# 32-bit products of zeros in TensorE's idle time in the first part of an attention and feed-forward kernel

## The chip, the cores and the metric

The kernel runs on one core of one Trainium2 chip. The metric is the device time of one execution, in microseconds. A profiled execution gives the trace: what each engine did, and what ended each of its waits. The engines are TensorE (PE, with its weight loads as PEld), VectorE (DVE), ScalarE (ACT), GpSimd (POOL) and SyncE (SP). SP and POOL also issue the DMAs.

## What is computed

Eight batches of eight heads, each with 512 local tokens and 32 global ones, 64 wide. Global queries attend to all 544 keys, local ones to the 32 global keys and to local keys at a distance of at most 32. The result, as 4352 rows of 512, goes through a feed-forward layer with a gate.

```python
k_all = np.concatenate([k_g, k_l], axis=2)
v_all = np.concatenate([v_g, v_l], axis=2)
out_g = np.matmul(sm(scale * np.matmul(q_g, k_all.transpose(0, 1, 3, 2))), v_all)
s_ll = scale * np.matmul(q_l, k_l.transpose(0, 1, 3, 2))
mask = np.abs(pos[:, None] - pos[None, :]) <= window
s_ll = np.where(mask, s_ll, -1000000000.0)
s_lg = scale * np.matmul(q_l, k_g.transpose(0, 1, 3, 2))
out_l = np.matmul(sm(np.concatenate([s_lg, s_ll], axis=-1)), v_all)
...
h = x @ w_in
g = h * np.clip(h + 3.0, 0.0, 6.0) / 6.0
return (g @ w_out).astype(np.float32)
```

## The kernel before

The attention of a batch is cut into four local units (`local`, L594) and two global ones (`globe`, L703). A local unit goes through the engines in this order:

- TensorE computes scores in 32x32 tiles, 64 products in one operation of the plan (L628 for the first two batches, L615 for the others), into the PSUM tiles `s`, or `m` for every second unit of the first batch.
- VectorE adds the mask and takes the maximum, one 128x128 block at a time (L644), and ScalarE takes the exponential (L650).
- TensorE transposes the eight blocks (L659, into `t` or `m`), and ScalarE or VectorE copies them to `et` (L306, L308).
- TensorE multiplies by the values (L673) into the one PSUM tile `a` of two banks. The unit's two halves take the first 264 columns of one bank each.
- VectorE divides by the row sums (L681, L682), reading both banks of `a` and writing `x`. TensorE transposes `x` (L695), and a copy puts it into `xt`.

The global units do the same with other shapes (L723, L731, L737, L748, L757). The feed-forward part of a batch is `first` (L801, ScalarE's L813, VectorE's gate L808) and `second` (L830, copied out in L838 and stored by SP). For the first batch `first` works on halves of 256 columns.

The order of all this is not written out. `Plan` (L38) holds a stream of operations for each step, each operation with the engine, its cost in microseconds and what it depends on. `lay` (L118) picks the operation that can start first, breaks ties by rank, keeps a clock for each engine, and returns one list; the program is emitted in that order (L919), so it is the order of each engine's queue. The planner counts TensorE's instructions (`count`, from 60 on; `n` is what an operation adds, a weight load and a product being two), because the instructions come in blocks of 256 (`BLOCK`) and a block that has been asked for takes time to come (`FETCH`, `stalls`). `mode` tells full products from tiled ones; a switch between them is costed at 0.097.

`setup` (L343) is a row of memsets on VectorE, first the masks, then the edges of `kt`, the ones and zeros of `v`, `vg` and `vs`. POOL issues the loads and builds the masks, and some of its work waits for these memsets: the load of `vg` (L447, issued in L296) waits for the memset of L351.

The semaphores are placed by the framework, from what each instruction reads and writes in a tile.

Of the kernel before, what the change touches and what calls it, by code (L numbers as in the profile page):

```python
# [9 lines left out]
FP32 = mybir.dt.float32  # L10
# [3 lines left out]
class Buf:  # L14
# [4 lines left out]
    def __init__(self, pool, readers):  # L19
        self.pool, self.at, self.slot, self.left, self.free_at = pool, None, None, readers, 0.0  # L20
# [17 lines left out]
class Plan:  # L38
# [4 lines left out]
    BLOCK = 256  # L43
    FETCH = 2.5
    SWITCH, ALONE = 0.097, 1.0
    SPARE, PHASES = 0.3, 9

    def __init__(self, pools, claims):
        self.count, self.fetched, self.mode = 60, 0.0, "full"
        self.claims = claims  # L50
        self.tune = TUNE
        self.issued = {}
        self.free = {p: [0.0] * n for p, n in pools.items()}
        self.streams = {}
        self.rank = {}
# [62 lines left out]
    def lay(self):  # L118
        at = self.at = {n: 0 for n in self.streams}
        clock = {}  # L120
        order = []
        total = sum(len(s) for s in self.streams.values())
        while len(order) < total:
            found, lone = [], []
            for n, ops in self.streams.items():
                if at[n] == len(ops):
                    continue
                op = ops[at[n]]
                t = self.ready(op, n)
                if t is None:  # L130
                    continue
                for e, cost in op.on.items():
                    start = max(t, clock.get(e, 0.0))
                    rank = self.rank[n](at[n]) if callable(self.rank[n]) else self.rank[n]
                    rank += self.tune.get((n, at[n] * self.PHASES // len(ops)), 0.0)
                    if e == "PE":
                        cost += self.switch(op)
                        if self.stalls(op, start, op.on[e])[0] > 0.2:
                            rank += 20
                        if op.mode[0] != "full" and self.mode != "full":  # L140
                            rank -= 15
                        elif op.mode[0] != "full" and start - t < self.ALONE:
                            lone.append(len(found))
                    found.append((start, rank, start + cost, n, e))
            if not found:
                raise RuntimeError("no operation can be laid: " + ", ".join(f"{n} {at[n]}" for n in at if at[n] < len(self.streams[n])))
            if len(lone) == 1:
                start, rank, end, n, e = found[lone[0]]
                found[lone[0]] = (start, rank + 12, end, n, e)
            first = min(found)  # L150
            e = first[4]
            here = [f for f in found if f[4] == e and f[0] <= first[0] + 0.03]
            start, _, end, n, e = min(here, key=lambda f: (f[1], f[0]))
            op = self.streams[n][at[n]]
            if len(op.on) > 1:
                start, end, e = min(((f[0], f[2], f[4]) for f in found if f[3] == n), 
                                    key=lambda f: f[1] + (self.SPARE + self.tune.get(("spare " + n, at[n] * self.PHASES // len(self.streams[n])), 0.0)
                                                          if f[2] == "DVE" else 0.0))
            for b, p, i in self.choose(op, n)[1]:
                b.at, b.slot = p, i  # L160
                self.free[p][i] = None
            at[n] += 1
            if op.landing is not None:
                self.issued.setdefault(e, []).append(op.landing)
            if e == "PE":
                wait, when = self.stalls(op, start, op.on[e])
                end += wait
                self.mode = op.mode[1]
                if self.count % self.BLOCK + op.n >= self.BLOCK:
                    self.fetched = when + wait + self.FETCH + min(6.0, max(0.0, clock.get("DMA", 0.0) - when - 1.0))  # L170
                self.count += op.n
            clock[e] = end
            op.end, op.engine = end + op.lat, e
            for b in op.reads:
                b.left -= 1
                b.free_at = max(b.free_at, op.end)
                if b.left == 0:
                    self.free[b.at][b.slot] = b.free_at
            order.append((start, n, op))
        return order  # L180
# [3 lines left out]
def kernel(  # L184
# [12 lines left out]
    nc = tc.nc  # L197
    P = 128
# [37 lines left out]
    def tiles(name, n, shape, dtype, pool=None):  # L236
        return [(pool or sb).tile(shape, dtype, tag=f"{name}{i}", name=f"{name}{i}") for i in range(n)]
# [37 lines left out]
    qn, kn = w_out_t[2], w_out_t[3]  # L275
    gts = [tiles(f"gts{r}_", NDFF, [P, Sl], FP16) for r in range(2)]

    mps = tiles("m", 3, [P, 512], FP32, pp)
    sps = tiles("s", 2, [P, 512], FP32, pp)
    tps = tiles("t", 1, [P, 1024], FP16, pp)  # L280
    aps = tiles("a", 1, [P, 2, 512], FP32, pp)

    plan = Plan(sizes, {})
# [28 lines left out]
    def turned(t):  # L312

        return tps[t.slot] if t.at == "t" else mps[t.slot].bitcast(FP16)

    state = {b: {} for b in range(B)}
    units = []
    made = {}

    def quarter(e, f):  # L320
        return slice((2 * e + f) * W, (2 * e + f + 1) * W)

    def pairs(t):

        return t.rearrange("p (c s b) -> p c s b", c=NC, b=2)
# [15 lines left out]
            nc.gpsimd.memset(lines(kt[r])[:, :, at:at + W], 0.0)  # L341

    def setup():  # L343
        nc.vector.memset(masks, 0.0)
        for r in range(2):
            for e in range(2):
                nc.vector.memset(pairs(kt[r])[quarter(e, 0), :, 0:W, :], 0.0)
                nc.vector.memset(pairs(kt[r])[quarter(e, 1), :, LINE - W:, :], 0.0)
            nc.vector.memset(v0[r][:, :, :, D:D1], 1.0)
            nc.vector.memset(vg[r], 0.0)  # L350
            nc.vector.memset(vg[r][0:W, :, D:D1], 1.0)  # L351
            nc.vector.memset(vs[r][0:W, 0, 0, :, :], 0.0)
            nc.vector.memset(vs[r][P - W:P, NU - 1, NJ - 1, :, :], 0.0)
# [528 lines left out]

    with tc.manual_schedule():
        setup()
        g_first(0)
        loads(0, "l0")
# [64 lines left out]
```

## Time and profile before

| What | Value |
|---|---|
| Time, three runs | 341.26, 340.41, 340.36 us; median 340.41 |
| The profiled execution | 341.78 us, its span 340.0 us |
| Mean granted TensorE clock | 0.999 |
| Products, weight loads on TensorE | 4456, 4456 |
| DVE, ACT, POOL busy | 75%, 71%, 45% of the span |
| First score product, the 60 after it | at 9.45 us, from 12.60 us |
| First L801, first L830 | at 29.32 us, at 55.25 us |
| DMA in the 40 slices | nine tenths or more in 17 of the first 26 |

The page gives the busy time of each engine, then the span in 40 slices of 8.5 us. The view of waits names who waited for whom, with the total, the number of times and the longest. The timeline lists instructions in order of time: start, length, engine, line, operation, result and operands, how many, and in brackets the idle time before them with what ended it. "issue" there is time in which the engine waited for nothing that the profile shows. The view by windows gives, for each stretch, the busy time of PE, PEld, DVE, ACT and POOL with the number of instructions, then the granted clock, the DMA share and GB/s.

### The profile page before, as it was taken

How to read it: one execution, taken by the hardware profiler on the slowest of the kernel's cores; microseconds unless marked ns; L12 is line 12 of the kernel's file. 1: busy time of each engine (PE TensorE's matmuls, PEld its weight loads, DVE VectorE, ACT ScalarE, POOL GpSimd, SP SyncE). 2: the span in 40 equal slices, each digit the busy share in tenths (PEclk: the TensorE clock that was granted, in tenths of full speed). 3: DMA queues.
4: the chain of work that ended last, by engine and by line, in shares of the span. 5: the costliest groups of instructions: out<-in, count | busy, mean ns of one | idle time of the engine just before them, and what ended most of it. 6: DMA issues, size and time to landing. Idle time of an engine off the chain costs nothing.

```text
span 340.0 us, 11227 instructions
## 1 busy us (share of the span) xinstructions
PE 312.2 (92%) x4456; PEld 169.3 (50%) x4456; DVE 255.2 (75%) x955; ACT 241.0 (71%) x572; POOL 152.3 (45%) x184
## 2 busy tenths in 40 slices
PE   0458969899999999999999999999999999999995
PEld 0335756544455445545554555554545554445654
DVE  7777897759889699968997999799889864443310
ACT  5578969756897797769967996888779743443331
POOL 8488579407954974394529376715600000000000
PEclk9999999999999999999999999999999999999999
DMA  7989999999981996499729939993100000010112
GB/s 123 171 149 160 185 228 170 174 225 155 208 133 38 166 191 82 81 158 184 173 41 171 191 75 92 114 202 70 64 7 31 33 31 34 31 62 33 62 42 85
DMA packets 107077, 39.28 MB, mean 116 GB/s; under 512 B 92368, under 2 KB 100816, under 8 KB 107024
## 3 DMA queue, kind: packets, MB, share of 16 engines
q0 software_dynamic: 93536, 17.44, 64.6%
q1 hardware_dynamic: 13488, 21.12, 23.5%
q8 instruction: 35, 0.57, 0.7%
q14 instruction: 18, 0.15, 0.2%
HBM read 35.39 MB, written 8.91 MB: 130 GB/s over the span
## 4 chain that ended last, share of the span: by engine, by line
PE 87%; DVE 6%; issue 2%; DMA 2%; POOL 1%; ACT 1%; POOLq 0%; DVEq 0%
PE m L830 35%; PE m L801 33%; PE t L659 5%; PE a L673 3%; PE s L615 2%; PE t L695 2%; DMA wout<-in_k_l_dram 2%; DVE gts L808 2%; PE s L715 1%; PE t L748 1%; PE s L628 1%; PE a L757 1%; DVE sm L644 1%; DVE kt L525 1%; DVE x L682 1%
## 5 line engine op out<-in xcount | busy, mean ns | idle before, releaser
L830 PE MATMUL m<-wout,gts 128*128 128x512 f16 (+1 forms) x560 | 134.9, 373 | 0.6 <-issue 0.6
L801 PE MATMUL m<-xt,win 128*128 128x512 f16 (+1 forms) x576 | 126.3, 359 | 4.0 <-DVE gts L808 3.5
L808 DVE SCALAR_TENSOR_TENSOR gts<-t,m 128x512 f16<-128x512 f32 (+1 forms) x160 | 94.7, 603 | 41.0 <-ACT t L813 39.9
L813 ACT ACTIVATE t<-m 128x512 f32<-128x512 f32 (+1 forms) x160 | 84.2, 532 | 40.4 <-PE m L801 36.8
L477 POOL COPY vs<-v 32x1056 f32<-32x1056 f32 (+3 forms) x80 | 77.5, 968 | 42.9 <-DMA v<-in_v_l_dram 39.2
L650 ACT ACTIVATE ex<-sm,mx 128x128 f16<-128x128 f32 x256 | 86.2, 393 | 10.3 <-DVE mx L644 9.8
L801 PEld LDWEIGHTS <-win 128*128 128x128 f16 x640 | 60.0, 98 | 55.2 <-issue 5.1
L830 PEld LDWEIGHTS <-gts 128*128 128x128 f16 x560 | 51.2, 98 | 48.9 <-issue 2.3
L644 DVE CUSTOM_DVE_ANT_0 sm<-s,mask 128x128 f32<-128x128 f32 x240 | 56.6, 285 | 7.2 <-PE s L628 3.8
L838 ACT COPY ot<-m 128x512 f32<-128x512 f32 (+1 forms) x35 | 20.0, 571 | 16.6 <-PE m L830 16.4
L296 POOL DMA_DIRECT2D rawq<-in_q_l_dram x12 | 12.6, 1059 | 36.5 <-DVE qt L562 22.0
L296 POOL DMA_DIRECT2D v<-in_v_l_dram x32 | 28.2, 891 | 1.0 <-DMA win<-in_moe_w_in_dram 1.0
L306 ACT COPY et<-t 128x1024 f16<-128x1024 f16 x18 | 18.2, 1012 | 9.7 <-PE t L659 9.7
L682 DVE TENSOR_TENSOR x<-a,rec 128x512 f16<-128x512 f32 x32 | 22.1, 691 | 1.1
L644 DVE DVE_READ_ACCUMULATOR2_ANT mx<- 128x1 f32 x256 | 21.2, 83 | 0.0
L659 PE MATMUL t<-ident,ex 128*128 128x128 f16 x256 | 20.9, 228 | 0.0
L659 PEld LDWEIGHTS <-ex 128*128 128x128 f16 x256 | 17.5, 102 | 6.1 <-issue 0.5
L628 PE MATMUL s<-kt,qt 32*32 32x128 f16 x384 | 5.8, 246 | 13.0 <-DVE kt L533 9.4
L562 DVE STREAM_TRANSPOSE qt<-rawq 128x512 f16<-128x512 f16 x24 | 15.9, 691 | 0.0
L566 DVE STREAM_TRANSPOSE kt<-rawk 128x512 f16<-128x512 f16 x24 | 15.5, 682 | 0.0
L731 DVE TENSOR_REDUCE top<-s 128x1 f32<-128x288 f32 x32 | 13.0, 446 | 3.3 <-PE s L723 2.5
L673 PE MATMUL a<-vs,et 128*32 128x65 f16 x1024 | 14.3, 197 | 1.0 <-issue 0.9
(81 smaller groups left out, 250.4 us busy)
## 6 DMA issues: line engine op xcount, KB each, us to landing
out_dram<-ot SPq DMA_DIRECT2D x31, 256.0 KB, 2.1
vs<-vg SPq DMA_DIRECT2D x32, 132.0 KB, 6.2
v<-in_v_l_dram POOLq DMA_DIRECT2D x32, 128.0 KB, 6.9
rawq<-in_q_l_dram POOLq DMA_DIRECT2D x12, 256.0 KB, 5.9
rawk<-in_k_l_dram POOLq DMA_DIRECT2D x12, 256.0 KB, 8.0
rawq<-rawq SPq DMA_DIRECT2D x12, 254.0 KB, 6.8
rawk<-rawk SPq DMA_DIRECT2D x12, 254.0 KB, 6.1
win<-in_moe_w_in_dram POOLq DMA_DIRECT2D x8, 256.0 KB, 6.7
```

What stands on the lines that cost most here:

```text
L296: eng.dma_start(out=o() if callable(o) else o, in_=i() if callable(i) else i)
L477: (nc.gpsimd if op.engine == "POOL" else nc.vector).tensor_copy(out=o(), in_=i())
L644: nc.vector.tensor_tensor_reduce(out=sms[sm.slot], in0=scored(c // 2)[:, z:z + P], in1=masks[:, m, :], scale=-scale, scalar=3.0e38, op0=AL ...
L650: nc.scalar.activation(out=exs[ex.slot][:, un, c, :], in_=sms[sm.slot], func=EXP, scale=-1.0, bias=mxs[mx.slot])
L659: nc.tensor.matmul(out=turned(tp)[:, z:z + P], lhsT=exs[ex.slot][:, un, c, :], rhs=ident, is_transpose=True)
L673: nc.tensor.matmul(out=o[quarter(e, f), un, c, 0:D + 1], lhsT=ets[et.slot][:, un, c, quarter(e, f) if b >= WORDS else quarter(e ^ (c // 2) ...
L682: nc.vector.tensor_tensor(out=xs[x.slot], in0=o[:, :, :, 0:D], in1=recs[rec.slot].to_broadcast([P, 2, NC, D]), op=ALU.mult)
L801: nc.tensor.matmul(out=o if len(x.shape) == 2 else o.rearrange("p (a c) -> p a c", a=2), lhsT=w_in_t[c // 8][:, m, (c % 8) * P:(c % 8 + 1) ...
L808: nc.vector.scalar_tensor_tensor(out=g, in0=shape(t1s[t1.slot][:, 0:n]), scalar=1.0, in1=shape(mps[ps.slot][:, 0:n]), op0=ALU.min, op1=ALU ...
L813: r = plan.add("t1", Op(("ACT", 0.09 + n * 0.00083), lambda: nc.scalar.activation(out=t1s[t1.slot][:, 0:n], in_=mps[ps.slot][:, 0:n], func ...
L830: nc.tensor.matmul(out=mps[ps.slot][:, 0:n], lhsT=gfn(c), rhs=w_out_t[c // 4][:, c % 4, cols], start=(c == 0), stop=(c == NDFF - 1))
L838: nc.scalar.copy(out=o, in_=i)
```

## The change

A tile `busy` of 128x248 zeros in FP32 is added and set to zero by VectorE ahead of the other memsets. A product `filler` of 128x128 weights and 248 columns, both from `busy`, writes the last 248 columns of the second bank of `a`; nothing reads them. When the planner lays an operation on TensorE that starts before 36 us on its clock, it puts as many fillers ahead of it as fit into the idle time since the last one (from 2.5 us for the first), at 0.6 us each and by half of that less. They add two each to the count of instructions, and nothing to the clock.

```diff
+    FILL, FIRST, UNTIL = 0.6, 2.5, 36.0
...
+        self.filler = None
...
             if e == "PE":
+                idle = start - clock.get(e, self.FIRST)
+                for _ in range(int(max(0.0, idle - self.FILL / 2) / self.FILL) if self.filler and start < self.UNTIL else 0):
+                    order.append((start, "fill", Op((e, self.FILL), self.filler, n=2)))
+                    order[-1][2].engine = e
+                    order[-1][2].end = start
+                    self.count += 2
+                    total += 1
+                    self.mode = "full"
                 wait, when = self.stalls(op, start, op.on[e])
...
+    busy = tiles("busy", 1, [P, 248], FP32)[0]
...
+    def filler():
+
+        nc.tensor.matmul(out=aps[0][:, 1, 512 - 248:512], lhsT=busy[:, 0:P], rhs=busy, start=True, stop=True)
+    plan.filler = filler
...
     def setup():
+        nc.vector.memset(busy, 0.0)
         nc.vector.memset(masks, 0.0)
```

## The prediction

> **What bounds the kernel now.** First the page: busy time by engine and the row of the granted clock.
>
> ```profile
> PE 312.2 (92%) x4456; PEld 169.3 (50%) x4456; DVE 255.2 (75%) x955; ACT 241.0 (71%) x572; POOL 152.3 (45%) x184
> PEclk9999999999999999999999999999999999999999
> ```
>
> TensorE sets the end, and 28 of 340 us are left to win. The throttle's row never falls, so by it there is nothing to warm up. Next, TensorE's waits in the first 60 us; past them it loses only 1.8 us by name.
>
> ```profile
> PE s L628 <- DVE kt L533: 9.4, 1, 9.4
> PE m L801 <- DVE gts L808: 3.5, 4, 1.7
> PE m L628 <- issue: 2.9, 1, 2.9
> PE s L628 <- DVE kt L525: 2.9, 1, 2.9
> PE m L695 <- DVE x L682: 2.3, 2, 1.3
> ```
>
> Then TensorE's timeline to 48 us, where like is compared with like.
>
> ```profile
> 12.60 1.29 PE L628 MATMUL s<-kt,qt 32*32 32x128 f16 x60 [2.85 <-DVE kt L525]
> ...
> 21.14 0.79 PE L628 MATMUL m<-kt,qt 32*32 32x128 f16 x41 [2.87 <-issue]
> ...
> 23.53 0.61 PE L695 MATMUL m<-ident,x 128*128 128x128 f16 x4 [1.04 <-DVE x L682]
> ...
> 27.99 0.61 PE L695 MATMUL m<-ident,x 128*128 128x128 f16 x4 [1.27 <-DVE x L682]
> 28.40 1.06 PE L659 MATMUL t<-ident,ex 128*128 128x128 f16 x8
> 29.32 2.72 PE L801 MATMUL m<-xt,win 128*128 128x256 f16 x12
> 31.97 0.43 PE L673 MATMUL a<-vs,et 128*32 128x65 f16 x32
> ...
> 36.36 0.61 PE L659 MATMUL t<-ident,ex 128*128 128x128 f16 x8
> 47.27 1.47 PE L801 MATMUL m<-xt,win 128*128 128x256 f16 x12 [1.66 <-DVE gts L808]
> 48.67 0.74 PE L628 MATMUL s<-kt,qt 32*32 32x128 f16 x64
> ```
>
> Twelve products of 256 columns take 2.72 us at 29 us and 1.47 at 47; eight transposes 1.06, later 0.61; 64 score products 1.28, later 0.74. So the array runs at about half rate up to some 31.9 us, under a row that says 9. What ended that was 2.65 us of unbroken full-array products (29.32 to 31.97).
>
> Last, the same stretch in windows (TensorE busy first, the granted clock third from the end).
>
> ```profile
> 12.00:16.00 4.00, 2.69 (x145) 1.92 (x152) 3.02 (x21) 2.65 (x10) 0.48 (x1) 1.00 1.81 170
> 16.00:20.00 4.00, 2.27 (x91) 1.60 (x76) 3.88 (x25) 3.75 (x10) 2.20 (x4) 1.00 1.25 192
> 20.00:24.00 4.00, 1.82 (x78) 1.46 (x78) 2.17 (x8) 3.29 (x8) 3.74 (x7) 1.00 0.71 128
> 40.00:44.00 4.00, 2.45 (x59) 1.97 (x58) 3.93 (x10) 3.17 (x8) 3.83 (x5) 1.00 1.65 194
> 44.00:48.00 4.00, 2.26 (x20) 1.93 (x20) 3.96 (x13) 2.25 (x8) 2.21 (x4) 1.00 1.18 245
> ```
>
> Small score products and transposes at 57 to 67% busy left the rate low for 16 us; full-array products at about the same share (40 to 48 us) held it high. From 37 to 51 us VectorE is full, and from 51.4 on TensorE. The end therefore moves by as much as the VectorE and ScalarE work of 24 to 37 us moves.
>
> **The change, part by part.** Edits to the plan's count only move the order; its order may change after each 256-instruction boundary. The two later waits on "issue" (0.9 and 0.6 us) bound that: plus or minus 0.7, taken as 0.
>
> *How many.* The planner is part of the kernel. Laid for the kernel before, its own gaps ahead of TensorE operations up to 36 us are 9.64 (from 2.5), 1.15 ahead of the third scores, 1.31 ahead of the first L673, 1.56 and 1.42 ahead of the first two L695; by the diff's rule, (gap - 0.3)/0.6 cut to a whole number, that is 15 + 1 + 1 + 2 + 1 = 20 products, 40 instructions in its count.
>
> *One product's price.* No 32-bit product is in the trace. From below: an f16 product of 256 columns, 1.47/12 = 0.12 us high, 2.72/12 = 0.23 low. From above: the diff's own 0.6, and at half rate 0.6 x 2.72/1.47 = 1.1. I take 0.6, by which the gaps were counted; operands twice as wide on both sides would make 2 x 2 f16 passes, 0.49 high and 0.91 low, on either side of it.
>
> *The memset.* The 128x264-word memset takes 0.28 us, so `busy` (248 words) about 0.26, ahead of everything on VectorE. It is not covered: POOL waits for VectorE's last memset of `vg`, and its loads and masks lead to the second K load, on the chain.
>
> ```profile
> 3.23 0.60 POOL L296 DMA_DIRECT2D vg<-in_v_g_dram  x1 [0.44 <-DVE vg L351]
> 25.03 1.01 ACT L306 COPY et<-t 128x1024 f16<-128x1024 f16 x1 [1.67 <-PE t L659]
> ```
>
> It is +0.26 at the first scores (12.60 to 12.86).
>
> *The first 15* start when `busy` is zero, near 1.3 us, and need 15 x 0.6 = 9 us, ended by 10.3; if the first six go at 1.1, by 13.3. The cover is the 12.4 us of idle before 12.60. Without it, every product over costs its length. I take 0.
>
> *Scores 1 to 3, 12.9 to 16.9 us.* If the rate is high here, they end up to 0.5 us sooner each, but VectorE reads each 128x128 block at 0.21 us one behind the other from 13.98 to 18.0 without a gap, then TensorE runs into the stall. Worth 0.
>
> *The stall.* TensorE stops after 223 products, 446 instructions; with the 60 that the plan counts ahead of them, about two blocks of 256. Sixteen added products (32 instructions) put the stop 16 score products sooner. Its end is set by the arrival of the next block of instructions, asked for 256 instructions earlier: 15 score products earlier (0.3 us), less the 0.26. I take its end unmoved; bounds -0.3 and +0.3. The 16 products run after it: 16 x 1.28/64 = +0.3.
>
> *One product ahead of the first L673.* The plan knows of no stall; after it there is no gap: +0.6.
>
> *Two ahead of the first L695, one ahead of the second.* They write columns 264 to 511 of the bank of `a` whose first 264 columns VectorE reads in L681 and L682. If the dependency is kept by bank, they wait for L682's end, when L695 itself could start: nothing fills the 1.04 and 1.27 us, and each costs its whole length, +1.2 and +0.6. If by bytes, they are hidden and cost 0. The trace has no second user of a bank to tell; I take the wait, as the tile is one and its bank is one. Behind them queue L695, the next unit's transposes L659, scores and L673; VectorE's copy to `xt` and ScalarE's `et` wait for those. The Trainium skill, PSUM — Partial Sum Buffer, on bank collisions, says that TensorE and a reader must be kept apart by bank and quadrant, not by address; by it the wait is there, and no run shown so far can say.
>
> *The rate after the stall.* Fillers raise it, I take it, within their 9 us. But from 13 to 28 us the array does what left it low before, with a few fillers in it and a stall of 2.87. I take it lost by 21 us. Nothing then gets shorter.
>
> *Sum.* To the second L695: 0.3 + 0.6 + 1.2 + 0.6 = +2.7. ScalarE is full from 25.03 to 38.6 but for idle of 0.27, 0.38 and 0.18; these 0.83 take up the delay. +2.7 - 0.83 = **+1.9 us** at 37 us, carried through VectorE's full stretch to the end. The profiled run took 341.78 us (span 340.0), 1.37 over the median of three; on that scale 343.7, on the median's 340.41 + 1.9 = **342.3**.
>
> **The rivals.**
>
> *The rate holds to 32 us, the fillers wait.* For: 40 to 48 us held it at 57 to 61% busy, and the stall is short. Against: that was full-array work. With the 0.49 of the high rate a product, after the stall: first L673 0.2 less, L695 0.2 less, L659 0.4 less, remaining scores 0.2 less, three fillers 1.47 more: +0.5 at ScalarE's 25.03; the second L695, L659 and the 12 products of L801 give 0.2 + 0.4 + 1.2 less and a filler 0.49 more, 1.3 less in all, but ScalarE's 0.83 of idle is all that can shrink: 0.5 - 0.83 = -0.3. About 340.1, no change. The Trainium skill, TensorE: Matmul & The Clock Gate, Part 1, gives this rule: full rate after about 3.4 us of activity, lost only after an idle window of that length. The 2.65 us at 29.32 agree with its rise; for its hold, the 2.87 us stall is too short.
>
> *The same, and the fillers are free* (hidden behind L682, or a fraction of 0.6). At 25.03 then -0.2 - 0.2 - 0.4 - 0.2 + 0.2 = -0.8, and -0.83 after it: -1.6, 338.8. For: the gaps are there. Against: the shared bank.
>
> *More than two instructions each.* With four, the stop comes 32 products sooner, after 191, so L659's eight transposes (ScalarE's `et` at 17.86) fall behind it. Then ScalarE starts `et` near 22.0 and has 1.01 + 0.40 + 1.92 + 1.57 + 0.63 to do before 25.03: 27.5, +2.5; with a filler wait on top and 0.83 off, some +2.9: 343.3. It decides from about 24 instructions more than planned (192 + 8 products done).
>
> *Zeros raise nothing.* Fifteen at 1.1 end at 17.8 in place of 12.86; the block is asked for later, too: +4, 344.5.
>
> **Chances.** Forecast 0.42; more instructions 0.13; zeros 0.05; rate held, waiting 0.20; rate held, free 0.20. About 0.3% (1.0 us) is what can be told from no change. Slower: 0.36 of the forecast, 0.13, 0.05 and 0.02 of the held rate: 0.56. Faster: 0.18 of the free case, 0.05 of the waiting one, 0.02 of order luck: 0.25. Same: 0.19. The forecast's own range is 340.8 (fillers at 0.23) to 344.2 (at 1.1). The range of 8 in 10 takes in most of the free case and the instruction case: 338.8 to 344.3.
>
> **What would show it.** Right: L659 at 1.06 and L801 x12 at 2.7 after 21 us as before; a filler starting at the end of L682 and L695 behind it; "issue" ending near 21.1. Wrong: L801 x12 at 1.4 from its first; fillers inside the gaps; a stall that ends elsewhere or a second one; a faster run with ScalarE's `et` before 25.0.

## The result

The changed kernel takes 1.0083 times the time of the kernel before, 95% interval 1.0056 to 1.0109: on the 340.41 us of the runs shown before, about +2.8 us. In eleven runs of each on one chip the medians are 344.14 and 341.09 us. It is slower, as forecast; the forecast was +1.9 us, 342.3, with a range of 338.8 to 344.3. The profiled execution took 345.36 us, its span 343.6.

In the changed kernel the lines are 17 further down: L645 is the scores (L628 before), L676 the transposes (L659), L690 the products with the values (L673), L699 the division (L682), L712 the transposes of `x` (L695), L818 and L847 the feed-forward products (L801, L830). L329 is the added product. The order of the other TensorE instructions is, product for product, that of the kernel before, in this kernel and in all the experiments.

First two rows of the page of the changed kernel, TensorE's busy time and the granted clock:

```profile
PE 324.0 (94%) x4496; PEld 178.8 (52%) x4496; DVE 255.4 (74%) x956; ACT 240.7 (70%) x572; POOL 152.3 (44%) x184
PEclk9756899999999999999999999999999999999999
```

TensorE is busy for 12 us more. It has 40 more products and 40 more weight loads, not 20: each 32-bit product is two of each, four instructions. And the clock row now shows a dip in its second to fifth slices.

TensorE's timeline of the changed kernel, to the first L847 (start, length, instructions, and the idle time before them with its cause):

```profile
1.18 8.69 PE L329 MATMUL a<-busy 128*128 128x248 f32 x30 [1.18 <-DVE busy L360]
...
14.98 1.19 PE L329 MATMUL a<-busy 128*128 128x248 f32 x2
16.11 1.05 PE L645 MATMUL s<-kt,qt 32*32 32x128 f16 x63
21.14 0.26 PE L645 MATMUL s<-kt,qt 32*32 32x128 f16 x1 [3.98 <-issue]
21.33 1.03 PE L676 MATMUL t<-ident,ex 128*128 128x128 f16 x8
...
23.28 1.20 PE L329 MATMUL a<-busy 128*128 128x248 f32 x2
24.41 0.63 PE L690 MATMUL a<-vs,et 128*32 128x65 f16 x32
26.08 2.02 PE L329 MATMUL a<-busy 128*128 128x248 f32 x4 [1.04 <-DVE x L699]
27.90 0.63 PE L712 MATMUL m<-ident,x 128*128 128x128 f16 x4
...
32.38 0.74 PE L329 MATMUL a<-busy 128*128 128x248 f32 x2 [1.47 <-DVE x L699]
32.92 0.63 PE L712 MATMUL m<-ident,x 128*128 128x128 f16 x4
...
34.23 2.47 PE L818 MATMUL m<-xt,win 128*128 128x256 f16 x12
...
59.92 2.75 PE L847 MATMUL m<-wout,gts 128*128 128x512 f16 x12
```

In the kernel before, the transposes and 23 more score products come ahead of the stall:

```profile
16.79 1.03 PE L659 MATMUL t<-ident,ex 128*128 128x128 f16 x8
17.75 0.52 PE L628 MATMUL m<-kt,qt 32*32 32x128 f16 x23
```

Three things stand here. The stall ends at 21.14, as before, but starts after 191 products of the kernel's own, all of them scores, and not after 223 (215 of scores and the eight transposes), so the eight transposes L676 lie behind it. The 32 products that are missing are the 30 and the 2 of the added ones ahead of the stall. The idle time of 1.04 us ahead of L712 is where it was, and the added products follow it. And L690, L712 and L676 take the long times of the kernel before (0.63, 0.63, 1.03). The second L712 starts at 32.92 (27.99 before), the first L818 at 34.23 (29.32 before), the first L847 at 59.92 (55.25 before): 4.7 us late at the start of the stretch that TensorE fills.

The windows of the changed kernel (TensorE's busy time first, the granted clock third from the end):

```profile
2.17:5.58 3.41, 3.41 (x10) 2.80 (x9) 2.70 (x16) 1.45 (x3) 2.58 (x11) 1.00 0.82 134
8.99:12.40 3.41, 1.05 (x9) 0.64 (x8) 2.35 (x7) 1.02 (x5) 3.41 (x6) 1.00 1.77 193
12.40:15.81 3.41, 2.97 (x126) 2.10 (x125) 2.44 (x17) 2.27 (x9) 0.34 (x1) 0.50 1.80 172
26.06:29.47 3.41, 3.39 (x24) 2.69 (x32) 2.18 (x13) 1.88 (x7) 3.41 (x6) 0.50 1.04 158
29.47:32.88 3.41, 1.25 (x50) 0.70 (x35) 2.73 (x14) 3.38 (x10) 2.27 (x3) 1.00 1.05 159
32.88:36.30 3.42, 3.42 (x23) 2.80 (x22) 1.87 (x10) 2.35 (x6) 1.63 (x2) 0.50 1.23 205
```

The trace's records of the clock change at 5.58 (up), 12.40 (down), 29.47 (up), 32.88 (down) and 36.30 (up for good); the windows are cut at these points. The products ahead of the scores raise the clock, and it falls 0.4 us before the first block of scores begins in earnest (12.78).

The longest waits of TensorE in the first 60 us of the changed kernel:

```profile
PE s L645 <- issue: 4.0, 1, 4.0
PE m L818 <- DVE gts L825: 3.6, 4, 1.7
PE s L645 <- DVE kt L542: 2.7, 1, 2.7
PE a L329 <- DVE x L699: 2.5, 2, 1.5
```

The waits for L699 are now those of the added products, not of L712: they wait for the same thing as the instruction behind them.

### The profile page after: what moved, and what is told of

Its sections match the earlier page's. It is cut to its first block, busy times and chain, and to the rows that moved or that the text cites. A ratio compares the mean times of both kernels' runs of the same rounds, so it can differ in the third digit from the quotient of the medians.

```text
span 343.6 us, 11308 instructions
## 1 busy us (share of the span) xinstructions
PE 324.0 (94%) x4496; PEld 178.8 (52%) x4496; DVE 255.4 (74%) x956; ACT 240.7 (70%) x572; POOL 152.3 (44%) x184
## 4 chain that ended last, share of the span: by engine, by line
PE 87%; DVE 6%; issue 2%; DMA 2%; POOL 1%; ACT 1%; POOLq 0%; DVEq 0%
PE m L847 35%; PE m L818 33%; PE t L676 5%; PE a L690 3%; PE s L632 2%; PE t L712 2%; DMA wout<-in_k_l_dram 2%; DVE gts L825 2%; PE a L329 1%; PE s L732 1%; PE s L645 1%; PE t L765 1%; PE a L774 1%; DVE kt L542 1%; DVE x L699 1%
## 5 line engine op out<-in xcount | busy, mean ns | idle before, releaser
L847 PE MATMUL m<-wout,gts 128*128 128x512 f16 (+1 forms) x560 | 134.9, 373 | 0.0
L818 PE MATMUL m<-xt,win 128*128 128x512 f16 (+1 forms) x576 | 126.0, 358 | 4.0 <-DVE gts L825 3.6
L830 ACT ACTIVATE t<-m 128x512 f32<-128x512 f32 (+1 forms) x160 | 84.2, 532 | 40.2 <-PE m L818 36.6
L818 PEld LDWEIGHTS <-win 128*128 128x128 f16 x640 | 60.0, 99 | 55.1 <-issue 5.1
L847 PEld LDWEIGHTS <-gts 128*128 128x128 f16 x560 | 51.2, 98 | 48.4 <-issue 1.8
L699 DVE TENSOR_TENSOR x<-a,rec 128x512 f16<-128x512 f32 x32 | 22.1, 691 | 1.1
L676 PEld LDWEIGHTS <-ex 128*128 128x128 f16 x256 | 17.5, 102 | 10.3 <-issue 4.9
L676 PE MATMUL t<-ident,ex 128*128 128x128 f16 x256 | 20.9, 228 | 0.0
L329 PE MATMUL a<-busy 128*128 128x248 f32 x40 | 13.9, 506 | 3.7 <-DVE x L699 2.5
L317 ACT COPY xt<-t 128x512 f16<-128x512 f16 x23 | 13.4, 584 | 2.2 <-PE t L712 2.1
```

The costliest lines, as they stand in the source:

```text
L317: nc.scalar.copy(out=o(), in_=i())
L676: nc.tensor.matmul(out=turned(tp)[:, z:z + P], lhsT=exs[ex.slot][:, un, c, :], rhs=ident, is_transpose=True)
L699: nc.vector.tensor_tensor(out=xs[x.slot], in0=o[:, :, :, 0:D], in1=recs[rec.slot].to_broadcast([P, 2, NC, D]), op=ALU.mult)
L818: nc.tensor.matmul(out=o if len(x.shape) == 2 else o.rearrange("p (a c) -> p a c", a=2), lhsT=w_in_t[c // 8][:, m, (c % 8) * P:(c % 8 + 1) ...
L830: r = plan.add("t1", Op(("ACT", 0.09 + n * 0.00083), lambda: nc.scalar.activation(out=t1s[t1.slot][:, 0:n], in_=mps[ps.slot][:, 0:n], func ...
L847: nc.tensor.matmul(out=mps[ps.slot][:, 0:n], lhsT=gfn(c), rhs=w_out_t[c // 4][:, c % 4, cols], start=(c == 0), stop=(c == NDFF - 1))
```

## The experiments

Each kernel is timed against the kernel before on the same chip; ratios are with 95% intervals. Single profiles differ by about a microsecond ahead of 20 us, with the landing of the second K load: the 60 scores started between 11.58 and 12.82 us in kernels where only that load held them. Three kernels have the same TensorE instructions up to 44 us: the kernel before, the one with the memset alone and the one with 40 small products near 45 us. In their profiles the stall ends at 21.14, 20.91 and 20.38, and the first product of the second feed-forward layer starts at 55.25, 55.70 and 53.97. So a difference of a microsecond or two between two profiles shows nothing by itself; the ratios do.

### The 15 products ahead alone

```diff
-    FILL, FIRST, UNTIL = 0.6, 2.5, 36.0
+    FILL, FIRST, UNTIL = 0.6, 2.5, 13.0
```

> Only the 15 products ahead of the first scores (60 instructions), none in the later gaps. Theory (each product is four instructions, so the stop for the next block comes 30 score products sooner, ahead of the eight transposes L659): 'issue' from about 16.9 to 21.1 us, the first copy to et at 22.2 to 22.5 instead of 17.9, the second L695 some 2 us later than in the kernel before (28.0), the end +1 to +2.5 us over before. Rival (only the products in the gaps cost, since the 15 end at 9.9 us, ahead of the scores): within 0.5 us of before.

Ratio 1.0036 (1.0010 to 1.0063), some +1.2 us, against the rival. In TensorE's timeline of this kernel the stop comes after one of the eight transposes:

```profile
16.09 0.29 PE L676 MATMUL t<-ident,ex 128*128 128x128 f16 x1
20.94 0.90 PE L676 MATMUL t<-ident,ex 128*128 128x128 f16 x7 [4.56 <-issue]
```

The first copy to `et` starts at 21.88, the second L712 at 30.24. Products that end at 10.5 us, ahead of all but the first four scores, cost 2 us of delay at 30 us.

### The same instructions without the array's work

```diff
-        nc.tensor.matmul(out=aps[0][:, 1, 512 - 248:512], lhsT=busy[:, 0:P], rhs=busy, start=True, stop=True)
+        half = busy.bitcast(FP16)
+        for _ in range(2):
+            nc.tensor.matmul(out=aps[0][0:W, 1, 512 - P:512], lhsT=half[0:W, 0:W], rhs=half[0:W, 0:P], start=True, stop=True)
```

(with `UNTIL` at 13.0, as above)

> In place of each of the 15 first products two f16 products of 32x32 by 128 columns, so 30 products and the same 60 instructions, with little array time and, I take it, no rise of the granted clock. Theory (instructions count, not the array's time): stall, et and end as in the run with only the first 15, within 0.7 us. Rival (the array's work or the clock's rise and fall costs): as the kernel before, within 0.5 us.

Ratio 1.0054 (1.0029 to 1.0078), as with the 15. The small products leave the clock down until 32.4 us, and the stop again falls after one transposition. Neither the array's time nor the clock's rise and fall is what the 15 cost, but their 60 places in the instruction stream.

### A whole block of instructions ahead

```diff
-    FILL, FIRST, UNTIL = 0.6, 2.5, 36.0
+    FILL, FIRST, UNTIL = 0.85, 2.5, 13.0
...
+    ahead = []
...
+        half = busy.bitcast(FP16)
+        for _ in range(0 if ahead else 108):
+            nc.tensor.matmul(out=aps[0][0:W, 1, 512 - 16:512], lhsT=half[0:W, 0:W], rhs=half[0:W, 0:16], start=True, stop=True)
+        ahead.append(1)
         nc.tensor.matmul(out=aps[0][:, 1, 512 - 248:512], lhsT=busy[:, 0:P], rhs=busy, start=True, stop=True)
```

(at 0.85 us each, ten 32-bit products fit in place of 15)

> Ahead of the first scores 108 small f16 products and then ten of the 32-bit ones, 216 + 40 = 256 instructions, none in the gaps. Theory (the place of the stop counts, not the products): a whole block is added, so TensorE stops after 223 products of the kernel again, L659 is done before, the first et at about 18, the second L695 at 28 to 28.5, the end within 0.6 us of before, though the clock is raised ahead of the scores and falls as with the 15. Rival (the rise and fall, or the array's work, costs): +1 us or more, as with the 15 alone.

Ratio 0.9994 (0.9960 to 1.0028): the cost is gone. The timeline of this kernel:

```profile
15.90 0.62 PE L681 MATMUL t<-ident,ex 128*128 128x128 f16 x8
16.45 0.44 PE L650 MATMUL m<-kt,qt 32*32 32x128 f16 x23
20.93 0.79 PE L650 MATMUL m<-kt,qt 32*32 32x128 f16 x41 [4.04 <-issue]
```

The stop is after 223 products again. Here the clock was up from 9.4 to 19.7 us, by its records, and scores and transposes took little more than half their time (0.62 for eight transposes against 1.03). What they saved went into the stall: 4.04 us for 2.87, ending within 0.2 us of where it did. The raised clock was worth nothing in this stretch.

### The five products in the gaps alone

```diff
-    FILL, FIRST, UNTIL = 0.6, 2.5, 36.0
+    FILL, FIRST, UNTIL = 0.6, 12.0, 36.0
```

> Only the five products in the later gaps (20 instructions). Theory (the product ahead of the first L673 and the three ahead of L695 run in front of what they precede, 0.83 us each at the low rate; the stop comes only two products sooner, so L659 is in time): the second L695 at 28.0 + 3.3 = 31.3 us, the end +1.5 to +2.5 us. Rival (the loss of the change is the block of instructions alone): +0.5 us or less.

Ratio 1.0070 (1.0041 to 1.0099), some +2.4 us: the larger part of the loss. The timeline of this kernel:

```profile
25.00 2.02 PE L329 MATMUL a<-busy 128*128 128x248 f32 x4 [1.04 <-DVE x L699]
26.82 0.63 PE L712 MATMUL m<-ident,x 128*128 128x128 f16 x4
```

VectorE's L699 starts at 24.26 and takes 0.69. The second L712 starts at 31.83, 3.8 us after that of the kernel before.

### The five products into a free PSUM tile

```diff
+                    spot = next((p, i) for p in ("t", "s", "m") for i, x in enumerate(self.free[p]) if x is not None and x <= start)
...
-    def filler():
+    def filler(spot):
...
+        to = {"t": tps[0].bitcast(FP32), "s": sps[0], "m": mps[spot[1]]}[spot[0]]
+        nc.tensor.matmul(out=to[:, 0:248], lhsT=busy[:, 0:P], rhs=busy, start=True, stop=True)
```

(on top of the edit above; the plan finds `t` free all five times)

> The five later products alone again, but into a PSUM tile that the plan has free, not into the bank of a that VectorE reads. Theory (they wait for L682 because of the bank): they start at the end of TensorE's work before, and the three ahead of L695 are hidden but for 1.66 - 1.04 = 0.6 us; second L695 at about 28.0 + 0.83 + 0.6 = 29.4, the end +0.3 to +1 us, at least 1 us below the run with the same five in the bank of a. Rival (the bank isn't what holds them, the queue is): the same as that run.

Ratio 0.9986 (0.9966 to 1.0007). In its timeline the four passes follow L692, the products with the values, at once:

```profile
22.69 0.63 PE L692 MATMUL a<-vs,et 128*32 128x65 f16 x32
23.25 2.02 PE L331 MATMUL t<-busy 128*128 128x248 f32 x4
25.07 0.63 PE L714 MATMUL m<-ident,x 128*128 128x128 f16 x4
```

The second L714 starts at 29.19, 2.6 us sooner than with the same products in `a`. Part of that is the clock, by its records up from 18.82 to 22.24 and from 25.65 us on here, and from 28.92 there. From the start of the products with the values to the first L714, at the low rate in both, it is 2.38 us here and 3.49 there (23.33 to 26.82): the 1.1 us are the wait. Writing into `a` is what held the products; the run changes the tile and the bank at once, so it does not tell which of the two the dependency is kept by. By the ratios, the two runs with these five products differ by more than the whole loss of the gaps. The end is a little better than forecast, since the raised clock stayed: L820 took 1.47 us for its first 12 products.

### The memset alone

```diff
-        nc.tensor.matmul(out=aps[0][:, 1, 512 - 248:512], lhsT=busy[:, 0:P], rhs=busy, start=True, stop=True)
+        pass
```

> The memset of busy stays and the plan counts its 20 products, but none is issued. Theory: the order of TensorE's instructions is that of before; the memset moves the first scores by at most 0.3 us and the end of the stall, the arrival of a block, by less; the end within 0.4 us of before. Rival (the memset's 0.26 us on the chain is carried through): +0.26 us, which this many runs can hardly tell from nothing.

Ratio 0.9993 (0.9956 to 1.0030): nothing that can be seen. As its TensorE instructions are those of the kernel before, its profile also shows what changes by itself. Its later waits on "issue" are this one alone, 0.61 us, where the kernel before has 0.85 + 0.57:

```profile
64.34 0.30 PE L690 MATMUL a<-vs,et 128*32 128x65 f16 x15 [0.61 <-issue]
```

### Moving the later stops

The changed kernel is 4.67 us late at the first L847 and only 3.6 at the end of the span, and its waits on "issue" after that point are 0.36 us, not 0.85 + 0.57. That looked like the merit of its 80 added instructions.

```diff
-        for _, _, op in plan.lay():
+        more = 40
+        for start, _, op in plan.lay():
+            if op.engine == "PE" and start > 43.0:
+                for _ in range(more):
+                    nc.tensor.matmul(out=aps[0][0:W, 1, 512 - 16:512], lhsT=busy, rhs=busy[:, 0:16], start=True, stop=True)
+                more = 0
             op.emit()
```

(on the kernel before, with a `busy` of 32x32 zeros in f16)

> The kernel before, with 40 small f16 products (80 instructions) put into TensorE's idle time near 45 us and no 32-bit ones. Theory (the change gets part of its loss back since its 80 instructions move the later stops for a block, 1.4 us in the kernel before and 0.4 in the changed one): the first 45 us as before, the later waits on issue 0.5 us or less in all, the end -0.7 to -1.2 us. Rival (the later waits have another cause, or the products take their place): within 0.4 us of before, or slower.

Ratio 1.0032 (0.9995 to 1.0070): the theory fell. The products filled the idle time near 45 us as meant, but of the later waits on "issue" in its timeline one grew:

```profile
61.84 0.36 PE L630 MATMUL s<-kt,qt 32*32 32x128 f16 x23 [0.37 <-issue]
69.14 0.81 PE L832 MATMUL m<-wout,gts 128*128 128x512 f16 x3 [2.79 <-issue]
```

The same number of added instructions gives 0.36 us of later stalls in a kernel that is 4.7 us late and 3.16 in one that is on time. So the place of a stop alone does not set its length. What ends it can be read from the packets of the instruction queue (q8, 16 KB each): in the kernel before and the changed one such a packet ends at 19.64 and 19.71 us, and in all 13 profiles each of the 33 waits on "issue" of TensorE's products ends 1.1 to 1.7 us after one. What sets when a packet moves was not tried by itself; the DMA traffic of the moment is a guess.

### Three products in a free tile, and the later stops

```diff
-                for _ in range(int(max(0.0, idle - self.FILL / 2) / self.FILL) if self.filler and start < self.UNTIL else 0):
+                for _ in range(int(max(0.0, idle - self.FILL / 2) / self.FILL) if self.filler and n == "xp" and start < self.UNTIL else 0):
...
+        more = 34
```

(on top of the free tile, which leaves two fillers ahead of the first L695 and one ahead of the second, and with the loop of the last experiment)

> Three 32-bit products alone, two ahead of the first L695 and one ahead of the second, into a free PSUM tile, and 34 small ones near 45 us (12 + 68 = 80 instructions). Theory: without the ones ahead of the scores and of L673 nothing is late ahead of 24 us; the products ahead of L695 fill idle time, but for some 0.6 us of the first two, and may raise the clock by 29 us; the later stops are moved as in the run with 40 small products: the end -1 to -2 us. Rival (the clock stays low, and the 0.6 us goes through): -0.5 us or less.

Ratio 1.0097 (1.0060 to 1.0135), the slowest of all, and against the theory. Up to 54 us it is as forecast: second L714 at 27.95, first L849 at 53.95. But the kernel with the 40 small products, which has none in the gaps and whose stall ends at the same time (20.38, here 20.36), is there at 53.97. Its lines, and then those of this kernel:

```profile
28.57 2.18 PE L803 MATMUL m<-xt,win 128*128 128x256 f16 x12
30.68 0.43 PE L675 MATMUL a<-vs,et 128*32 128x65 f16 x32
...
29.28 1.47 PE L820 MATMUL m<-xt,win 128*128 128x256 f16 x12 [0.49 <-ACT xt L318]
30.68 0.43 PE L692 MATMUL a<-vs,et 128*32 128x65 f16 x32
```

In these two profiles the raised clock wins back what the three products cost, and no more. Then come waits on "issue" of 1.21 and 2.52 us, and the second one does more than delay. The windows of this kernel around it:

```profile
66.90:70.31 3.41, 0.89 (x5) 0.29 (x3) 1.31 (x4) 0.98 (x3) 0.00 (x0) 1.00 0.96 245
70.31:73.72 3.41, 3.41 (x18) 2.02 (x17) 0.00 (x0) 1.49 (x4) 0.00 (x0) 0.50 0.76 182
```

With TensorE idle for 2.5 of 3.4 us the clock fell, and the next window ran at half.

### Versions from these parts

The three products ahead of L695 in the free tile, without the small ones at 43 us:

> Only the three products ahead of the first two L695, into a free PSUM tile (12 instructions); nothing ahead of the scores and nothing near 45 us. Theory: second L695 no later than before but for 0.6 us, the clock raised by about 26 to 29 us, L801 x12 at 1.5 us; the end 0 to -1.5 us. What differs from the run with 34 small products near 45 us, +1.0% there, is then the later waits on issue (3.7 us there). Rival (the three products themselves cost): slower than before by 1 us or more.

Ratio 0.9970 (0.9941 to 0.9999). The same with 108 small and ten 32-bit products, one block, ahead of the scores:

```diff
-        for _, _, op in plan.lay():
+        order = plan.lay()
+        zero = busy.bitcast(FP16)
+        for _ in range(108):
+            nc.tensor.matmul(out=aps[0][0:W, 1, 512 - 16:512], lhsT=zero[0:W, 0:W], rhs=zero[0:W, 0:16], start=True, stop=True)
+        for _ in range(10):
+            nc.tensor.matmul(out=aps[0][:, 1, 512 - 248:512], lhsT=busy[:, 0:P], rhs=busy, start=True, stop=True)
+        for _, _, op in order:
             op.emit()
```

> The change with both of its costs taken out: a whole block of 256 instructions ahead of the scores (108 small products and ten 32-bit ones), and in the gaps only the three ahead of the first two L695, into a free PSUM tile. Theory (a raised clock has little to win here, since ahead of 21 us VectorE and the stall set the pace and behind it ScalarE): no stall or wait worse than in the kernel before up to 50 us, the twelve products of L801 near 29 us at 1.5 instead of 2.7 us, the end 0 to -1.5 us. Rival (the raised clock is worth what TensorE's busy time loses, some 5 us): -3 us or more.

Ratio 0.9961 (0.9936 to 0.9987): the change with both its costs taken out, and with them two of its five products in the gaps, is a little faster than the kernel before. In its timeline the second L714 and the first L820 show the raised clock:

```profile
28.25 0.40 PE L714 MATMUL m<-ident,x 128*128 128x128 f16 x4 [0.74 <-DVE x L701]
29.58 1.47 PE L820 MATMUL m<-xt,win 128*128 128x256 f16 x12 [0.49 <-ACT xt L318]
```

L820 now waits for ScalarE, and starts no sooner than before (29.32): its 12 products are 1.2 us shorter than in the profile of the kernel before, and 0.7 shorter than in that of the kernel with 40 small ones. The two versions can't be told apart, so the part ahead of the scores is not shown to be worth anything; where their 0.3 to 0.4% comes from is open. With 101 small products ahead in place of the block (`range(101)`, and no 32-bit ones there):

> The three products ahead of L695 in a free tile and 101 small ones (202 instructions) ahead of the scores, so that the stop moves from 223 to about 250 products, 27 score products later, and is asked for as much later. Theory (end of the stall set by when the block is asked for, 27 score products at 20 ns): stall begins 0.5 us later and ends 0 to 0.5 us later; up to 50 us -0.5 to 0 against the run without them; what the later waits on issue do can't be told ahead, so the end within 2 us of it either way.

Ratio 1.0006 (0.9978 to 1.0034). The stop did move to 250 products, and the stall shrank to 2.02 us. But it ended at 20.36, 1.3 us sooner than without the small products (21.67), where the theory had the same time or later. With profiles that differ by about as much, this does not bear the theory out, and does not refute it. Later waits of 0.92 and 1.41 us took back what was won.

### What the profiles add up to

The first feed-forward product of the second layer (L830 before), the span from it to the end, and the waits on "issue" in that span, from the profiles:

| Kernel | First L830 | From it to the end | Later waits on issue | Difference |
|---|---|---|---|---|
| before | 55.25 | 284.8 | 1.42 | 283.3 |
| changed | 59.92 | 283.7 | 0.36 | 283.3 |
| 15 ahead | 57.46 | 283.4 | 0.28 | 283.1 |
| five in gaps | 58.89 | 284.0 | 0.60 | 283.4 |
| five in gaps, free tile | 55.20 | 284.4 | 1.10 | 283.3 |
| whole block | 55.71 | 285.2 | 1.98 | 283.2 |
| memset alone | 55.70 | 283.9 | 0.61 | 283.3 |
| 40 small at 43 us | 53.97 | 286.4 | 3.16 | 283.3 |
| three, free tile, 34 small | 53.95 | 288.7 | 3.73 | 284.9 |
| block and three, free tile | 54.25 | 285.3 | 1.97 | 283.3 |
| three, free tile | 54.69 | 284.7 | 1.37 | 283.4 |

From the first L830 on, every kernel takes 283.1 to 283.4 us and its later stalls (the two not shown 283.2 and 283.0); the one exception is the kernel whose clock fell at 70 us, by 1.6. So the time is set by two things: when the second layer starts, and how long TensorE waits for instructions after it. The changed kernel is 4.67 us worse in the first and 1.06 better in the second, 3.6 in its span. The second is not shown to be the change's doing: the kernel with the memset alone is 0.81 better there, too, with the TensorE instructions of the kernel before.

## Why the prediction was right, and where its terms were off

- *Half rate under a row that says 9.* Right, and now seen in the records: the first one of the kernel before is the rise at 32.03 us, and the row counts the time ahead of the first record as full. In the changed kernel, too, it is 1.00 in the window 2.17 to 5.58, where a pass of the 32-bit product takes 0.41 us.
- *The first 15 end in time.* Right: at 9.87, before the scores.
- *The rate is lost by 21 us.* Right, and sooner than thought: at 12.40, ahead of the 60 scores. So what lost it was not the small scores and the stall, as the prediction had it, but the idle time behind the added products (1.05 us busy from 8.99 to 12.40); scores and stall come later.
- *Fillers wait for L682 and run in front of L695.* Right; the run in the free tile shows that writing into `a` is the cause, though not whether tile or bank counts. The Trainium skill, PSUM — Partial Sum Buffer, on bank collisions, asks for a separation by bank, and the trace fits it: 1.04 us of idle with the product in the bank of `a`, none in another.
- *One product's price, 0.6.* Mis-sized. Four passes take 2.02 us and two 1.20 at the low rate, so a pass is 0.41 and a product 0.82; at the high rate 19 passes took 4.1 us, 0.43 a product. The terms of the four products between the stall and the second L695 were 0.6 + 1.2 + 0.6 = 2.4 us; at these prices they are 0.82 + 1.65 + 0.43 = 2.9. In the timeline what stands behind them starts 1.13, 1.82 and 0.54 us after they do, 3.5 in all.
- *Two instructions each.* This is the step that failed. "Sixteen added products (32 instructions) put the stop 16 score products sooner" was 64 instructions and 32 products, as the rival with 0.13 had it: a stop after 191. So L659 fell behind the stall. That rival's mechanism is the one that ran, and its 343.3 is the figure nearest to the result (340.41 x 1.0083 = 343.2), although ScalarE's second `et` came at 29.42 and not at its 27.5. In the forecast the term was +0.3; the 15 alone, with no filler behind them, put the second L695 2.2 us late, and with a whole block ahead, L659 in front of the stall again, that delay was gone. The delay there was +2.7 in the sum and 4.9 in the trace.
- *ScalarE's idle 0.83 takes up delay.* Wrong: 4.93 us late at the second L695, 4.67 at the first L830; 2.25 and 2.21 for the 15 alone. Those gaps end with transposes and products that are just as late: in the changed kernel ScalarE still waits 0.32 and 0.35 us there, and 0.40 more for L712.
- *Carried to the end.* In the two profiles 1.1 us of the delay came back, as the later stalls fell from 1.42 to 0.36; the forecast allowed 0.7 either way. Most of that can be chance, as the memset alone shows (0.61).
- So that +1.9 came near +2.8 is in part luck. The delay at 37 us was over twice the forecast, 4.9 us in the profile; at the end the profiles differ by 3.6 and the runs by 2.8, and nothing in the sum stands for what was lost on the way.
- *The memset and the stall's end.* Right within what can be seen: 21.14 in both profiles, where equal instructions gave 20.38 to 21.14, and the memset alone gives no difference.

## What to carry to other kernels

Count a filler in instructions before you count it in time: ahead of a stop for instructions, each one moves useful work behind it, even in time that is idle. A filler must not write into a PSUM tile that another engine is still reading, or it waits for the very thing that made the gap and then stands in front of the work. Compare a profile with a second one of the same instructions before reading a microsecond in it. And ask what the faster engine waits for next: where another engine or the stream of instructions sets the pace, a doubled clock is only a longer wait.

## What the runs showed of the hardware

- A 32-bit product of 128x128 by 248 columns is two weight loads and two passes, 0.82 us at the low rate and 0.43 at the high one. The Trainium skill, FP8 and Floating Point Precision, "TensorE Precision Notes", speaks of four passes; in time that agrees (four f16 passes of 256 columns are 0.91 and 0.49), in instructions the trace shows two.
- The clock changes in steps of 3.41 us: 5.58, 12.40, 29.47, 32.88, 36.30 are 2, 5, 1 and 1 steps apart. The Trainium skill, TensorE: Matmul & The Clock Gate, Part 1, has this window. Its rule that the rate is lost after an idle window does not cover what these traces show: the clock fell after a window in which TensorE was busy for 1.25 of 3.41 us, and after another with 1.05.
- Busy time alone is not what raises it. The whole-block kernel and the one with 40 small products near 45 us had these windows, both at the low rate (the column shows 1.00 because their first record, the rise, comes later, at 9.42 and 30.06):

```profile
2.59:6.01 3.42, 3.42 (x67) 3.09 (x64) 2.74 (x15) 1.43 (x4) 2.59 (x11) 1.00 0.99 134
26.65:30.06 3.41, 2.82 (x20) 2.36 (x21) 2.53 (x14) 3.13 (x8) 3.41 (x6) 1.00 1.10 193
```

The first, busy throughout but with small 32x32 products up to 4.2 us, left the clock low; the second, with transposes and 128x128 products, raised it. Nor is it busy time alone that keeps it: the clock stayed up through 1.74 us in the changed kernel (49.95 to 53.36) and fell after 1.86 in the kernel with 101 small products (24.20 to 27.61). What counts is not shown.

- A wait on "issue" of TensorE's products is a wait for a block of instructions: the page of the kernel before has 35 packets in q8 for 8912 products and weight loads, 255 each; 60 added instructions moved the stop by 30 products and 256 by none; and each such wait ended 1.1 to 1.7 us after a packet.
- A stall for instructions can lower the clock: 2.52 us of it at 67 us was followed by 3.41 us at half rate, which made that kernel 1.6 us longer than its stalls explain. The kernel before may have such drops, too: in 22 of its 98 runs beside the experiments the mean granted clock was 0.994 or 0.995, which is what 3.41 us at half rate make of 340, and the median time 344.0 us; in the other 76 the median was 341.3.
